# V of a batch's 64-row tail from two halves side by side in one stationary operand, and query weights staged in two parts

## Chip, cores and metric

The kernel runs on one core of one Trainium2 chip. The metric is the device time of one execution in microseconds; the runs shown are summarised by their median. The profile is of one further execution of the same program.

## What is computed

Three stages follow each other, for 8 batches of 576 positions. Retention attention gives x; a mixture of four attention experts with a gate that keeps two of them gives a new x; a token and channel mixing stage gives the output. Only the middle stage's projections of x matter here:

```python
logits = x @ w_gate                      # 512 -> 4
for e in range(E):                       # E = 4, head width 64
    q = x @ wq[e]; k = x @ wk[e]; v = x @ wv[e]
    scores = scale * (q @ k.transpose(0, 2, 1))
    ...                                  # causal softmax a, row sums
    ye = a @ v @ wo[e]
```

Products need more precision than one fast pass gives. So each operand is kept as two arrays, a rounded high part (h) and the remainder (l), and a product is three passes: h·h, h·l and l·h.

## The kernel before, in words

**Tiling.** The 576 positions of a batch are five chunks of 128, 128, 128, 128 and 64 rows (`ROWS`); the last one is the tail. `ret_values` (L164) makes x of one chunk in PSUM. VectorE scales it into `xt` (L190), ScalarE rounds it into `xh` (L192), and GpSimd subtracts the two into `xl` (L193). `xh` and `xl` hold a whole batch, four tiles of 128 contraction rows by 576 columns, with one buffer each (`XT`, L187). The routine ends by issuing, on SyncE's DMA queue, the loads of the chunk four places on (`loads`, L194 to L196).

**Projections.** `proj_qk` (L234) makes q or k of two experts for half of the positions; the weights are the stationary operand there. `proj_v` (L261) makes V and the gate's logits of one chunk: the stationary operand is the chunk of `xh` or `xl`, the moving operand is the 260 columns of V and gate weights. There are three passes of four contraction tiles, so 12 matmuls of 260 columns, for the 64-row tail (chunk 4, "v4") as for a 128-row chunk. ScalarE then copies the 256 columns of V (L276) and the 4 logits (L277) out of PSUM. `gate` (L279) works on the logits with a series of short VectorE instructions.

**Order.** TensorE's order is written out by hand. `SLOTS` (L45) says what goes beside each of the ten attention units of a batch; the next batch's tail is made in slot 8 ("R5") and its projections "v3 k01 v4 g" come in slot 9, so v4 is followed by that batch's gate. `ret_first` and `work` calls from L538 on do the same for batch 0, before attention starts. The other engines' queues are ordered by the framework's planner; TensorE's outputs go round a ring of eight PSUM buffers (`w`, `WB`).

**Weights.** The projection weights come in two staging tiles of the pool `w1s`: V and gate columns (512 to 772, `load_w1(512, NW1)`, L452), and the query and key columns (0 to 512, `load_w1(0, 512)`, L455) behind the first four chunks' loads. Of these, columns 0 to 256 serve the first pair of experts (k00, q00, k01), 256 to 512 the second (Q01, K10 and on, in attention's first slots). `split_w1` (L448) makes WH with ScalarE (L106) and WL with VectorE (L107), for the first 512 columns in four steps after the third chunk (L560 to L562). The pool is given back at L563.

Of the kernel before, what the change touches and what calls it, by code (L numbers as in the profile page):

```python
# [10 lines left out]
F32 = mybir.dt.float32  # L11
F32R = mybir.dt.float32r
# [3 lines left out]
AF = mybir.ActivationFunctionType  # L16
# [4 lines left out]
B, H, S, D = 8, 8, 576, 64  # L21
E, DM = 4, 512
# [4 lines left out]
NV = E * D + E  # L27
# [36 lines left out]
def tile_kernel(ctx: ExitStack, tc: tile.TileContext, qk, kv, w1, wo, wot, wd, cst, out):  # L64
    nc = tc.nc
    consts = ctx.enter_context(tc.tile_pool(name="consts", bufs=1))

    def pool(name, **kw):
        return tc.alloc_tile_pool(name=name, bufs=1, **kw)
# [11 lines left out]
    w1p = pool("w1p", side="right")  # L81
# [13 lines left out]
    WH = w1p.tile([128, 4, NW1], F32R, name="WH")  # L95
    WL = w1p.tile([128, 4, NW1], F32R, name="WL")
# [8 lines left out]
    def split(h, l, src):  # L105
        nc.scalar.activation(h, src, AF.Copy)  # L106
        MARK["split"] = nc.vector.tensor_sub(l, src, h)  # L107
# [24 lines left out]
    def half(x):  # L132
        return slice(x * 64, x * 64 + 64)
# [30 lines left out]
    def ret_values(b, c):  # L164

        R = ROWS[c]
        t, vp = QKT[b, c], VP[b, c]
        px = ps1.tile([128, 4, R], F32, name="w", bufs=WB, padded_shape=[128, 4, 128])
        for j in range(R // 64):
            sm = SM.pop((b, 2 * c + j))  # L170
            for x in range(4):
                for s in range(2):
                    nc.tensor.matmul(px[half(1 - s), x, half(j)], vp[half(s), j, x, :], sm[half(s), x, :],
                                     start=j == 0 and x == 0, stop=False, skip_group_check=True)
                yield
        for j in range(R // 64):
            k = 2 * c + j
            for x in range(4 if k else 0):
                for s in range(2):
                    nc.tensor.matmul(px[half(1 - s), x, half(j)], SB[k % 4][half(s), x, :], t[half(s), x, half(j)],  # L180
                                     start=False, stop=False, skip_group_check=True)
                yield
        for x in (QKT, KVT, VP):
            x.pop((b, c))
        cs = slice(c * C, c * C + R)
        if c == 0:
            XT[b] = (w1p.tile([128, 4, S], F32R, name="xh", bufs=1),  # L187
                     w1p.tile([128, 4, S], F32R, name="xl", bufs=1))
        xt = ret.tile([128, 4, R], F32, name="xt", bufs=2, padded_shape=[128, 4, 128])
        MARK["xt"] = nc.vector.tensor_mul(xt, px, gt[:, :, cs])  # L190
        xh, xl = XT[b]
        MARK["xh"] = nc.scalar.activation(xh[:, :, cs], xt, AF.Copy)  # L192
        MARK["xl"] = nc.gpsimd.tensor_sub(xl[:, :, cs], xt, xh[:, :, cs])  # L193
        nx = (b, c + LDB) if c + LDB < NCH else (b + 1, c + LDB - NCH)  # L194
        if nx[0] < B:
            loads(*nx)  # L196
# [64 lines left out]
    def proj_v(b, c):  # L261
        xh, xl = XT[b]
        if c == 0:
            VB[b] = att.tile([128, NCH, E, D], F32, name="V", bufs=2)
        V = VB[b]
        l = LG[b % 2]
        w0 = 512
        R = ROWS[c]
        cs = slice(c * C, c * C + R)
        ps = ps1.tile([128, NV], F32, name="w", bufs=WB, padded_shape=[128, 512])  # L270
        for x, W in ((xh, WH), (xh, WL), (xl, WH)):
            for kt in range(4):
                nc.tensor.matmul(ps[:R], x[:, kt, cs], W[:, kt, w0:w0 + NV], start=x is xh and W is WH and kt == 0,  # L273
                                 stop=x is xl and kt == 3)
        pv = ps[:R, :E * D].rearrange("p (e d) -> p e d", e=E)
        nc.scalar.copy(V[:R, c, :, :], pv)  # L276
        nc.scalar.activation(l[:R, c, :], ps[:R, E * D:], AF.Copy)  # L277
# [26 lines left out]
    def work(b, names):  # L304
        for n in names.split():
            x = b + n.islower()
            if x < B:
                if n in "Gg":
                    gate(x)
                elif n[0] == "T":  # L310
                    token_tile(ps1, 0, len(X2))
                elif n[0] == "F":
                    fuse(int(n[1]))
                elif n[0] in "Vv":
                    proj_v(x, int(n[1]))
                else:
                    proj_qk(x, int(n[1]), int(n[0] in "Kk"), int(n[2]))
# [94 lines left out]
    w1s = pool("w1s")  # L412
# [28 lines left out]
    wst = {}  # L441

    def load_w1(a, z):
        wst[a] = w1s.tile([128, 4, z - a], F32, name=f"wst{a}", bufs=1)
        nc.sync.dma_start(wst[a], w1.rearrange("(k p) n -> p k n", p=128)[:, :, a:z])

    def split_w1(a, k):
        t = wst[a]  # L448
        sl = slice(a, a + t.shape[2])
        split(WH[:, k, sl], WL[:, k, sl], t[:, k])  # L450

    load_w1(512, NW1)  # L452
    for c in range(1, LDB):
        loads(0, c)
    load_w1(0, 512)  # L455
    nc.sync.dma_start(tie, cst[:, o + 1088:o + 1088 + E * E].rearrange("p (a b) -> p a b", a=E))
    nc.sync.dma_start(ident, cst[:, 0:128])

# [73 lines left out]
    def fuse(p):  # L532
        acc = ps1.tile([128, DM], F32, name="w", bufs=WB)
        for kt, (th, wt) in enumerate(FW):
            mm3(acc, wt[:, 0, p, :], wt[:, 1, p, :], th[:, 0, :], th[:, 1, :], kt == 0, kt == 3)
        split(MH[:, p, :], ML[:, p, :], acc)
# [3 lines left out]
    for k in range(2):  # L540
        with tc.issue_after(MARK["xt"].ins), tc.issue_after(MARK["xh" if k else "S"].ins):
            split_w1(512, slice(2 * k, 2 * k + 2))
    with tc.issue_after(MARK["xl"].ins):
        scale()
    warm_up(WARM2)
# [13 lines left out]
    ret_first(0, 2, (0, 3), [(6, 7)])  # L559
    for k in range(4):  # L560
        with tc.issue_after(MARK["xt"].ins), tc.issue_after(MARK["xh"].ins):
            split_w1(0, k)  # L562
    w1s.release()  # L563
    work(-1, "v1")
    ret_first(0, 3, (0, 4), [(8,)])
    work(-1, "v2 k00")
# [86 lines left out]
    for t in range(nu + 1):  # L653
        b, k = divmod(t, 10)
        if b < B - 1:
            more, between, after = *SLOTS[k], ""
        else:
            b = B - 1
            more, between, after = LAST[t - 10 * b]
        if t < nu:  # L660
            at_scores(units[t])
            work(b, more)
            if units[t][2] == NCH - 1:
                at_norm(*units[t][:2])
        if t == nu - 1:
            assert not jobs[1]
            cvt.release()
            atk.release()
            zp = pool("zp")
        if between == "O":  # L670
            for o in outs:
                at_out(*o)
            outs = []
        ready, new = outs, []
        if t:
            at_trans(units[t - 1])
            ub, up, um = units[t - 1]
            if GROUPS[GRP[um]][-1] == um:
                new.append((ub, up, GRP[um]))
        outs = new  # L680
        if b < B - 1:
            if between[:1] == "R":
                c = int(between[1])
                x = b + 1
                def mid():
                    for o in ready:
                        at_out(*o)

                ret_step(x, c - 1, mid)
            else:  # L690
                outs = ready + outs
        else:
            work(b, between)
            for o in ready if t < nu else ready + outs:
                at_out(*o)
        work(b, after)


        i = int(t >= JOBS[0])
        x = t - JOBS[0] if i else t - 2  # L700
        while jobs[i] and (x + 1) / due[i] >= njobs[i] - len(jobs[i]) + 1 - 1e-6:
            with ExitStack() as es:
                for e in ("dve", "act"):
                    es.enter_context(tc.issue_after(MARK[e].ins))
                jobs[i].pop(0)()
        if t == nu - 11:
            assert not jobs[0]
            ret.release()
            w2 = pool("w2")
            WOH, WOL, MH, ML = [w2.tile([128, 2, DM], F32R, name=x) for x in ("WOH", "WOL", "MH", "ML")]  # L710
            wol = pool("wol")
            wa = pool("wa")
            fuse_load()
            load_o(0)
            load_o(1)
        if t == nu - 10:
            fuse_split(4)
        if t == nu - 8:
            fuse_split(0)
        if t == nu - 7:  # L720
            w1p.release()
            wa.release()
            w2b = pool("w2b")
            TK = w2b.tile([128, 9, 2, S], F32R, name="TK")
            wk1 = pool("wk1")
            for kt in KORD:
                nc.sync.dma_start(TK[:, kt].bitcast(F32), TD[kt])
# [257 lines left out]
```

## Time and profile before

| What | us |
|---|---|
| median of 3 runs | 880.44 |
| lowest and highest of the 3 | 877.99, 881.26 |
| the profiled execution | 879.58 |
| its span | 877.8 |

The span reaches from the first to the last instruction; 1.8 us of the profiled execution lie around it. TensorE is named PE in the profile (PEld for its weight loads), VectorE DVE, ScalarE ACT, GpSimd POOL and SyncE SP. "Idle before" is the time an engine stood still ahead of an instruction, with the work that ended last before it started; "issue" there means that the profile shows nothing it waited for.

### The profile page before, as it was taken

How to read it: one execution, taken by the hardware profiler on the slowest of the kernel's cores; microseconds unless marked ns; L12 is line 12 of the kernel's file. 1: busy time of each engine (PE TensorE's matmuls, PEld its weight loads, DVE VectorE, ACT ScalarE, POOL GpSimd, SP SyncE). 2: the span in 40 equal slices, each digit the busy share in tenths (PEclk: the TensorE clock that was granted, in tenths of full speed). 3: DMA queues.
4: the chain of work that ended last, by engine and by line, in shares of the span. 5: the costliest groups of instructions: out<-in, count | busy, mean ns of one | idle time of the engine just before them, and what ended most of it. 6: DMA issues, size and time to landing. Idle time of an engine off the chain costs nothing.

```text
span 877.8 us, 25574 instructions
## 1 busy us (share of the span) xinstructions
PE 859.2 (98%) x10072; PEld 795.2 (91%) x10072; DVE 622.0 (71%) x1729; ACT 454.6 (52%) x1258; POOL 218.7 (25%) x268
## 2 busy tenths in 40 slices
PE   6999999999999999999999999999999999999998
PEld 6989889888888989898789999999989999999998
DVE  4588787878788886876678777676377665766632
ACT  1366667666666766666576445353244533444320
POOL 3325253443525453341300012010210103001010
PEclk9899999999999999999999999999999999999999
DMA  9857677676867676548674442422525233241411
GB/s 317 246 155 239 171 221 199 194 224 187 255 169 222 202 211 179 160 108 238 185 265 170 83 111 47 120 37 61 141 57 139 62 96 93 34 124 25 100 34 54
DMA packets 140440, 130.30 MB, mean 148 GB/s; under 512 B 75808, under 2 KB 114976, under 8 KB 140320
## 3 DMA queue, kind: packets, MB, share of 16 engines
q1 hardware_dynamic: 140176, 128.39, 52.6%
q8 instruction: 79, 1.29, 0.6%
q0 software_dynamic: 144, 0.28, 0.2%
q14 instruction: 41, 0.34, 0.1%
HBM read 78.03 MB, written 32.00 MB: 125 GB/s over the span
## 4 chain that ended last, share of the span: by engine, by line
PE 88%; DMA 4%; DVE 3%; ACT 1%; issue 1%; POOL 1%; SPq 0%; ACTq 0%; DVEq 0%; POOLq 0%
PE acc L787 22%; PE w L245 11%; PE w L101 6%; PE w L102 6%; PE w L103 6%; PE w L335 6%; PE w L273 6%; PE w L401 5%; PE w L382 5%; PE w L787 3%; PE w L158 3%; PE w L143 3%; DMA kt<-qk 2%; DMA KK<-KN 1%; PE w L180 1%
## 5 line engine op out<-in xcount | busy, mean ns | idle before, releaser
L787 PE MATMUL acc<-TK,zh 128*128 128x288 f32 (+2 forms) x896 | 156.4, 296 | 0.5 <-ACT ob L405 0.5
L787 PEld LDWEIGHTS acc<-TK,zh 128*128 128x128 f32 x896 | 132.1, 189 | 1.2 <-issue 0.6
L343 ACT ACTIVATE P<-P,st 128x128 f32<-128x128 f32 (+4 forms) x160 | 95.4, 598 | 42.2 <-DVE st L338 41.9
L803 POOL TENSOR_TENSOR ul<-u,uh 128x576 fp32r<-128x576 f32 x16 | 24.2, 1531 | 309.6 <-ACT uh L802 309.6
L787 PE MATMUL acc<-TK,zl 128*128 128x288 f32 (+1 forms) x448 | 95.9, 295 | 0.0
L106 ACT ACTIVATE zh<-cs 128x512 fp32r<-128x512 f32 x64 | 40.3, 630 | 76.6 <-PE acc L787 61.4
L335 PE MATMUL w<-KK,U 128*64 128x288 f32 (+4 forms) x384 | 76.6, 327 | 1.5 <-DMA KK<-KN 1.4
L107 DVE TENSOR_TENSOR zl<-cs,zh 128x512 fp32r<-128x512 f32 x64 | 45.1, 705 | 43.2 <-ACT zh L106 42.5
L338 DVE CUSTOM_DVE_ANT_0 P<-w,cm 128x128 f32<-128x128 f32 (+4 forms) x160 | 71.1, 477 | 4.8 <-PE w L335 3.9
L787 PEld LDWEIGHTS acc<-TK,zl 128*128 128x128 f32 x448 | 72.4, 189 | 0.0
L626 ACT ACTIVATE cs<-cs,quarter 128x256 f32<-128x256 f32 x72 | 36.5, 507 | 55.4 <-DVE cs L624 55.2
L629 DVE SCALAR_TENSOR_TENSOR cs<-cs,x 128x512 f32<-128x512 f32 x72 | 50.7, 706 | 20.1 <-ACT cs L627 19.4
L382 PE MATMUL w<-ident,P 128*128 128x128 f32 (+2 forms) x480 | 60.1, 260 | 1.6 <-DVE sm L147 1.3
L335 PEld LDWEIGHTS w<-KK,U 128*128 128x128 f32 (+1 forms) x384 | 54.0, 171 | 8.0 <-DVE nwt L355 1.5
L193 POOL TENSOR_TENSOR xl<-xt,xh 128x512 fp32r<-128x512 f32 (+1 forms) x40 | 47.8, 1195 | 45.4 <-ACT xh L192 45.4
L479 POOL TENSOR_TENSOR r<-r,ex 128x192 f32<-128x192 f32 (+1 forms) x51 | 29.5, 578 | 116.2 <-ACT hl L480 42.0
L192 ACT ACTIVATE xh<-xt 128x512 fp32r<-128x512 f32 (+1 forms) x40 | 23.5, 589 | 66.9 <-DVE xt L190 66.8
L103 PE MATMUL w<-uh,CH 128*128 128x288 f32 x192 | 56.6, 295 | 0.0
L102 PE MATMUL w<-ul,CH 128*128 128x288 f32 x192 | 56.5, 294 | 0.0
L101 PE MATMUL w<-uh,CH 128*128 128x288 f32 x192 | 56.5, 294 | 0.0
L401 PE MATMUL w<-PT,V 128*64 128x192 f32 (+3 forms) x576 | 56.4, 325 | 0.0
L382 PEld LDWEIGHTS w<-ident,P 128*128 128x128 f32 (+2 forms) x480 | 47.1, 138 | 8.3 <-DVE sm L147 2.7
(153 smaller groups left out, 2340.4 us busy)
## 6 DMA issues: line engine op xcount, KB each, us to landing
KK<-KN SPq DMA_DIRECT2D x128, 144.0 KB
kt<-qk SPq DMA_DIRECT2D x32, 512.0 KB
kv<-kv SPq DMA_DIRECT2D x32, 512.0 KB
raw<-wd SPq DMA_DIRECT2D x43, 192.0 KB
xd<-xb SPq DMA_DIRECT2D x126, 64.0 KB
out<-u SPq DMA_DIRECT2D x28, 288.0 KB
u<-xd SPq DMA_DIRECT2D x28, 288.0 KB
td<-hl SPq DMA_DIRECT2D x27, 192.0 KB
```

The source lines that it names most:

```text
L101: nc.tensor.matmul(ps, ah, bh, start=first, stop=False)
L102: nc.tensor.matmul(ps, ah, bl, start=False, stop=False)
L103: nc.tensor.matmul(ps, al, bh, start=False, stop=last)
L245: nc.tensor.matmul(ps, W[:, kt, w0:w0 + 128], x[:, kt, sl], start=x is xh and W is WH and kt == 0, stop=x is xl and kt == 3)
L273: nc.tensor.matmul(ps[:R], x[:, kt, cs], W[:, kt, w0:w0 + NV], start=x is xh and W is WH and kt == 0, stop=x is xl and kt == 3)
L335: nc.tensor.matmul(ps[s][:R], U[:, s, rs], KK[:, s, x, j0:j1], start=x == 0, stop=x == 1)
L338: MARK["dve"] = nc.vector.tensor_tensor_reduce(Ps[s][:R, j0:j1], ps[s][:R], cm[:R, o + j0:o + j1], 1.0, st[:R, 0, s:s + 1] if i else 3.0e3 ...
L343: MARK["act"] = nc.scalar.activation(Ps[s][:R, :n], Ps[s][:R, :n], AF.Exp, bias=st[:R, last, s:s + 1], scale=-1.0, accum_out=SUM[p][:R, m, ...
L382: nc.tensor.transpose(tp[:w, j, :], Ps[s][:R, j * C:j * C + w], ident[:R, :R])
L401: nc.tensor.matmul(po[s * 64:s * 64 + 64, c0:], V[:ROWS[j], j, 2 * p + s, :], v, start=j == 0, stop=j == last, skip_group_check=True)
L629: nc.vector.scalar_tensor_tensor(z, cs, -1.0, x2[:, None, ds].to_broadcast([128, 2, 256]), op0=OP.mult, op1=OP.mult)
L787: nc.tensor.matmul(acc[d][j], A[:, dc], TK[:, kt, W, t0:t1], start=q == 0 and n == 0, stop=q == 8 and n == 2)
```

## The change

For the tail, `xl` becomes 64 columns wider. ScalarE writes the rounded tail of x a second time, into these columns, right behind the tail of `xl`, so that the two tails stand side by side as 128 columns. `proj_v` of the tail then takes these 128 columns as the stationary operand and makes two passes, with WH and WL, 8 matmuls of 260 columns. Rows 0 to 63 of the result hold the product of xl's tail, rows 64 to 127 that of xh's tail. ScalarE copies the upper rows to an SBUF tile `vt`, and VectorE adds this to the lower rows, once for V and once for the logits. The product of the two low parts, which was left out before, is now in the sum.

The staging tiles of the weights become two buffers of one name, each of 260 columns. Columns 0 to 256 are loaded where 0 to 512 were; columns 256 to 512 are loaded into the first buffer, after the V weights in it have been split. The four split steps stay where they were, with 2 contraction tiles of 256 columns each in place of one of 512. The pool `vtp` takes the place of the staging pool and is given back with `ret`.

```diff
@@ ret_values
-                     w1p.tile([128, 4, S], F32R, name="xl", bufs=1))
+                     w1p.tile([128, 4, S + 64], F32R, name="xl", bufs=1))
...
         MARK["xl"] = nc.gpsimd.tensor_sub(xl[:, :, cs], xt, xh[:, :, cs])
+        if R == 64:
+            nc.scalar.activation(xl[:, :, S:], xt, AF.Copy)
@@ proj_v
+        if R == 64:
+            for W in (WH, WL):
+                for kt in range(4):
+                    nc.tensor.matmul(ps, xl[:, kt, S - 64:], W[:, kt, w0:w0 + NV], start=W is WH and kt == 0,
+                                     stop=W is WL and kt == 3)
+            t = vtp.tile([64, NV], F32, name="vt", bufs=1)
+            nc.scalar.activation(t, ps[64:], AF.Copy)
+            tv, pv = [x[:, :E * D].rearrange("p (e d) -> p e d", e=E) for x in (t, ps[:64])]
+            nc.vector.tensor_add(V[:64, c, :, :], pv, tv)
+            nc.vector.tensor_add(l[:64, c, :], ps[:64, E * D:], t[:, E * D:])
+            return
@@ load_w1
-        wst[a] = w1s.tile([128, 4, z - a], F32, name=f"wst{a}", bufs=1)
+        wst[a] = w1s.tile([128, 4, z - a], F32, name="wst", bufs=2, padded_shape=[128, 4, NV])
@@ the startup
-    load_w1(0, 512)
+    load_w1(0, 256)
...
             split_w1(512, slice(2 * k, 2 * k + 2))
+    load_w1(256, 512)
...
-            split_w1(0, k)
+            split_w1(k // 2 * 256, slice(k % 2 * 2, k % 2 * 2 + 2))
     w1s.release()
+    vtp = pool("vtp")
...
             ret.release()
+            vtp.release()
```

## Rows read from the trace of the kernel before

**Rows 1.** The page: span, busy time by engine, share of the span, instructions.
```profile
span 877.8 us, 25574 instructions
PE 859.2 (98%) x10072; PEld 795.2 (91%) x10072; DVE 622.0 (71%) x1729; ACT 454.6 (52%) x1258; POOL 218.7 (25%) x268
```

**Rows 2.** Busy time by stretch: start:end, length, each engine's busy time, granted clock.
```profile
0.00:45.00 45.00, 37.20 (x801) 35.21 (x802) 22.93 (x48) 12.99 (x34) 15.72 (x24) 0.92 0.87 280
45.00:96.00 51.00, 50.66 (x875) 45.75 (x875) 42.13 (x144) 33.25 (x109) 20.24 (x28) 1.00 0.66 189
...
352.00:404.00 52.00, 51.74 (x811) 46.75 (x811) 41.30 (x145) 34.36 (x115) 18.38 (x28) 1.00 0.51 137
```

**Rows 3.** The chain that ended last: share of the span by engine.
```profile
PE 88%; DMA 4%; DVE 3%; ACT 1%; issue 1%; POOL 1%; SPq 0%; ACTq 0%; DVEq 0%; POOLq 0%
```

**Rows 4.** Waits of PE over the span: in total, times, longest.
```profile
PE w L180 <- issue: 4.0, 2, 2.9
...
PE w L382 <- DVE sm L147: 1.3, 5, 0.3
```

**Rows 5.** That chain in batch 0's startup: start, length, work.
```profile
38.06 1.44 PE w L273 x12
39.50 1.60 PE w L245 x12
41.10 1.44 PE w L273 x12
42.53 0.39 PE w L335 x4
```

**Rows 6.** That chain around v3, k01, v4 of batch 1.
```profile
83.95 1.43 PE w L273 x12
85.38 1.82 PE w L245 x12
87.20 1.43 PE w L273 x12
```

**Rows 7.** The tail's matmuls and loads, by form, 38 to 45 us.
```profile
L273 PEld LDWEIGHTS w<-WL,xh x8: 133/160/190, 38.3 to 41.6; 128*128 128x128 f32 x4, 128*64 128x64 f32 x4
```

**Rows 8.** ACT in time order: tail rounding, tail V and logits.
```profile
35.98 0.42 ACT L192 ACTIVATE xh<-xt 128x256 fp32r<-128x256 f32 x1 [1.53 <-DVE xt L190]
...
42.57 0.36 ACT L276 COPY V<-w 64x256 f32<-64x256 f32 x1 [1.02 <-PE w L273]
42.84 0.17 ACT L277 ACTIVATE lg<-w 64x4 f32<-64x4 f32 x1
```

**Rows 9.** DVE in time order: an add from PSUM, then the gate's start.
```profile
31.80 0.41 DVE L162 TENSOR_TENSOR S<-w,S 128x256 f32<-128x256 f32 x1
...
43.03 0.18 DVE L282 TENSOR_REDUCE gmx<-lg 128x5 f32<-128x20 f32 x1 [1.00 <-ACT lg L277]
```

**Rows 10.** All engines in time order around batch 1's v4.
```profile
85.62 0.74 POOL L193 TENSOR_TENSOR xl<-xt,xh 128x256 fp32r<-128x256 f32 x1
...
85.86 0.78 ACT L343 ACTIVATE P<-P,st 64x576 f32<-64x576 f32 x1 [0.77 <-DVE st L338]
...
89.14 0.17 DVE L282 TENSOR_REDUCE gmx<-lg 128x5 f32<-128x20 f32 x1 [0.41 <-ACT lg L277]
...
94.00 0.93 DVE L259 SCALAR_TENSOR_TENSOR U<-w,U 64x288 fp32r<-64x288 f32 x2 [0.86 <-ACT U L256]
...
94.45 0.82 PE L382 MATMUL w<-ident,P 64*128 64x64 f32 x10
```

**Rows 11.** SyncE's DMA issues in time order: weights, then the loads behind.
```profile
7.88 0.43 SPq L445 DMA_DIRECT2D wst<-w  x1
...
14.58 0.33 SPq L120 DMA_DIRECT2D kv<-kv  x1
21.22 0.33 SPq L117 DMA_DIRECT2D kt<-qk  x1
```

**Rows 12.** The weight splits at startup in time order: V's last, then 512 columns.
```profile
11.73 1.35 DVE L107 TENSOR_TENSOR WL<-wst,WH 128x520 fp32r<-128x520 f32 x1 [0.62 <-ACT WH L106]
...
27.22 2.17 ACT L106 ACTIVATE WH<-wst 128x512 fp32r<-128x512 f32 x4
...
27.87 4.01 DVE L107 TENSOR_TENSOR WL<-wst,WH 128x512 fp32r<-128x512 f32 x4 [1.22 <-ACT WH L106]
```

**Rows 13.** PE resuming after two startup gaps, in time order.
```profile
20.74 0.27 PE L180 MATMUL w<-kt,S 64*64 64x64 f32 x2 [2.85 <-issue]
...
25.07 0.37 PE L180 MATMUL w<-kt,S 64*64 64x64 f32 x2 [1.17 <-issue]
```

**Rows 14.** Busy time up to each gap, and the stretches behind (columns as above).
```profile
0.00:17.90 17.90, 14.11 (x349) 12.86 (x350) 8.03 (x13) 3.91 (x7) 6.04 (x15) 1.00 0.92 318
...
0.00:23.90 23.90, 17.27 (x476) 15.83 (x476) 11.28 (x19) 4.54 (x8) 8.07 (x17) 0.95 0.94 310
...
20.00:25.00 5.00, 3.16 (x127) 2.96 (x126) 2.89 (x6) 0.63 (x1) 1.90 (x2) 0.64 0.97 275
25.00:30.00 5.00, 4.93 (x108) 4.68 (x109) 3.16 (x4) 3.04 (x7) 2.61 (x2) 0.67 0.72 186
```

**Rows 15.** Instruction queue: whole span (packets, MB), then from 18 to 19 us.
```profile
q8 instruction: 79, 1.29, 0.6%
...
q8 instruction: 1, 0.02, 7.0%
```

## The prediction

> **What bounds the kernel now.** I read the page's busy times first: TensorE is busy for 859.2 of 877.8 us, and no other engine passes 71% [rows 1]. An average can hide stages, so the busy time by stretch comes next. Before attention starts TensorE idles for 45.0 - 37.2 = 7.8 us; in a whole batch of attention, 45 to 96 us, for 0.34 us, and in the last one that still projects, 352 to 404 us, for 0.26 us [rows 2]. The chain that ended last says the same, with 88% of it on TensorE [rows 3]. The waits name what is left: the largest by far is 4.0 us of "issue" in two gaps at startup, and the largest on another engine's work in the attention stage is 1.3 us in five pieces [rows 4]. So a matmul taken out of attention should come off the time nearly whole, and an instruction added to another engine costs only what it makes TensorE wait. The startup is a case of its own.
>
> **Part 1, four matmuls fewer in each tail.** In the chain, v3 (128 stationary columns) takes 1.44 us from 38.06 to 39.50 and v4 (64 columns) 1.44 us from 41.10 to 42.53, 12 matmuls each [rows 5]; in batch 1 the two take 1.43 us each [rows 6]. That is 119 ns a matmul, and a full stationary operand costs no more than a half one. So the tail's 8 matmuls of 128 columns take 8 x 119 = 0.95 us in place of 1.43, 0.48 us less, and in eight batches 8 x 0.477 = 3.8 us. All eight tails lie before 404 us, seven of them inside full attention slots and batch 0's in a stretch where the chain goes from matmul to matmul. Each moves work behind it up by as much.
>
> The weight loads do show the width: 133 ns at the least for 64 columns, 188 to 190 ns for 128 [rows 7]. They lie beside the matmuls, so I cost the difference at nothing; the cover is the 119 ns pitch, which both widths hold. Were the loads what sets the pitch, 8 x 188 = 1.50 us against 12 x 133 = 1.60 us would leave 0.1 us a batch, 0.8 us in all. The Trainium skill ("TensorE: Matmul & The Clock Gate", section "LDWEIGHTS (loading the stationary operand)") says that a load takes as many cycles of 1.2 GHz as it has columns, and this speaks against the change: by it, as an estimate, eight loads of 107 ns are 0.21 us more than twelve of 53 ns, 1.7 us more over eight batches if loads set the pace. The trace agrees that width lengthens a load, with other numbers, but the equal 1.44 us say that here the load does not end last.
>
> **Part 2, the second writing of xh's tail.** One ScalarE instruction of 128x256 elements a batch, like the first writing, 0.42 us [rows 8], 3.4 us in all. Queued behind it is the exponential of the tail's attention unit, which before stood 0.77 us idle for VectorE at this place; and GpSimd's xl tail, which v4 needs too, ends only at 85.62 + 0.74 = 86.36, after the copy would (from 85.1 to 85.5) [rows 10]. So it is hidden, at nothing. Without that cover it would cost 0.42 us a batch.
>
> **Part 3, getting V out of PSUM.** Before: ScalarE 0.36 us for V and 0.17 us for the logits [rows 8]. After: one ScalarE copy of 64x260, about 0.37 us, then on VectorE an add of 256 columns from PSUM, about 0.41 us by the 128x256 add, and an add of 4 columns, about 0.18 us by the gate's first short instruction [rows 9]. The trace has no such add of 64 rows and 4 columns, hence "by". VectorE gets 0.6 us more a batch, 4.7 us in all. The new wait is VectorE's for ScalarE's copy; queued behind it are the gate and the next units' score reductions. Before, the gate waited there too, 1.00 us in batch 0 and 0.41 us in batch 1 [rows 9, 10], and since the logits' own ScalarE copy drops out, the gate starts at about +0.3 us. Later VectorE has a pause of 0.86 us at 93.1 to 94.0, where it waits for ScalarE's part of U [rows 10], and there the delay ends. The PSUM buffer is held for some 0.5 us longer; its next user is the eighth output after v4, the transposes at 94.45, six microseconds after v4's end at 88.6 [rows 6, 10]. Bounds of part 3: 0 if all is covered, 8 x 0.6 = 4.7 us if every added VectorE instant reaches TensorE. The trace is near the lower end (1.3 us for all such waits of five pieces); I take 0.3 us.
>
> **Part 4, weights in two parts.** The first half, 512 KB, is issued where 1 MB was, at 7.88 us. The second waits for the last split of the V weights, 11.73 + 1.35 = 13.08 us; on SyncE's queue it stands behind the tail's kv load at 14.58 us, so it goes out at about 15 to 16 us, and the load behind it is not due before 21.22 us [rows 11]. It is wanted by ScalarE's third split, about 27.22 + 2 x 0.54 = 28.3 us [rows 12], some 12 us later. The bytes are the same, the four steps split the same number of elements, so ScalarE's 2.17 us and VectorE's 4.01 us stay [rows 12]. k00, q00 and k01 need only the first two steps now, some 2 us earlier than before, but TensorE was not waiting there. Cost: nothing in the likely case.
>
> What can move is the supply of instructions. TensorE's 20,144 instructions came in 79 packets [rows 1, 15], about 255 each, some 128 matmuls with their loads. The two "issue" gaps of 2.85 and 1.17 us [rows 13] stand at the 349th and the 476th matmul, 127 apart, and while TensorE stood in the first, one such packet moved between 18 and 19 us [rows 14, 15]. So I read them as waits for the next packet while the data loads fill the DMA engines (shares of 0.92 and 0.94 [rows 14]). Behind the first gap the granted clock falls to the lower level, 1.2 GHz: means of 0.64 and 0.67 in two stretches of 5 us are 3.6 + 3.3 = 6.9 us of it [rows 14]; less the second gap that is 5.7 us of work at half speed, which costs about 2.9 us more. The Trainium skill ("Runtime: NRT & Kernel Launch", section "Instruction fetch mechanics") has the same 256-instruction blocks but says that fetching is hidden by the time instructions take to issue; here the rows show 4 us that were not. Early in the startup half a megabyte less now stands in the queue, in rows of 1 KB and not 2 KB, and the rest follows behind. I can't say which way a packet's place moves; bounds are -4.0 us (both gaps gone), -7 us with the clock, and +3 us (the first gap again). I take 0.
>
> **Sum.** -3.8 + 0.3 = -3.5 us. The profiled execution's 879.58 us (span 877.8 and 1.8 around it) gives 876.1; it lies 0.86 us below the median of 880.44, which gives 876.9. The mean of the three runs and the profiled one is 879.8, so I say **876.2**.
>
> **The rivals.**
> (a) The startup's instruction wait shrinks. For it: smaller pieces ahead of the packet. Against: the same bytes fill the queue at 15 to 20 us. Half of the gaps and of the clock's loss would be -3.5 us: 872.7; the case spans 870 to 875.
> (b) The saving is given back: the added 0.6 us of VectorE in each batch shows as a wait of the next transposes, or the packet comes later. Half of 4.7 us is 2.4: 878.6, span 877.6 to 881. Against it are the pauses named in part 3.
> (c) Loads set the pitch once they are wide, so only 0.8 us is saved: 879.0. Here the change doesn't do what it says. The skill's rule of part 1, worked out with its own figures, would make it 1.7 us slower. The equal 1.44 us speak against both.
> (d) Slower: the second half of the weights lands late, because its issue waits for a free staging buffer behind SyncE's other loads. ScalarE and VectorE then stand in the third split, and x of the fourth chunk, queued behind it on VectorE, is late for TensorE. It decides from a landing at 28.3 us; for a loss of over 0.5% it has to eat 3.8 + 4.4 = 8.2 us, a landing at about 36.5 us. At 40 us: 28.3 to 40 is 11.7, less 3.8: 888. The 12 us of margin speak against it.
>
> **How the numbers follow.** 0.5% of 880.44 is 4.4 us, about what a measurement of this kernel can tell from no change; faster means below 876.0. My forecast has 0.55 and spans 874.8 to 877.6, split by that bound into 0.20 faster and 0.35 same. (a) has 0.22, all faster; (b) 0.14 and (c) 0.04, same; (d) 0.05, slower. So faster 0.42, same 0.53, slower 0.05. For 8 in 10, I leave out the lower third of (a), the upper third of (b), part of (c) and all of (d): 872.8 to 879.8.
>
> **What would show it.** Right: each L273 group of the tail has 8 matmuls in about 0.95 us; TensorE's busy time is some 3.8 us lower; its waits in attention stay under 1 us a batch; VectorE's gate starts at most 0.6 us later behind v4. Wrong: tail groups at 140 ns or more a matmul (c); a new wait of transposes or scores on VectorE in each batch (b); other "issue" gaps or clock in the first 30 us (a or b); an idle ScalarE ahead of the third split (d).

## The result, and the profile after

The changed kernel takes 886.72 us (median of 7, 881.91 to 887.82) against 878.72 us for the kernel before in the same comparison: a ratio of 1.0076 [1.0049, 1.0103] (ratios here are of the means, with 95% intervals). By the medians it is slower by 8 us; the forecast was 876.2, and its range ended at 879.8. The profiled execution took 886.5 us, 6.9 us more than the profiled one of before (879.58).

The page's busy times (as in [rows 1]) and the chain's shares by engine (as in [rows 3]) show at once that TensorE got no more work: it has the 32 matmuls fewer that were meant. VectorE has the 16 short instructions more, and ScalarE is busy 3.3 us longer, as forecast (3.4). What grew is "issue", from 1% to 2% of the chain. TensorE's busy time isn't the 3.8 us lower that was named as a sign of being right: it is 859.5 us after 859.2. Work at the lower clock counts as busy for longer, 1.4 us of it at startup and up to 1.7 us behind 275 us (both below); the rest was not traced.

```profile
span 884.7 us, 25540 instructions
PE 859.5 (97%) x10040; PEld 795.7 (90%) x10040; DVE 623.1 (70%) x1745; ACT 457.9 (52%) x1258; POOL 219.6 (25%) x268
...
PE 90%; DMA 3%; issue 2%; DVE 2%; SPq 1%; POOL 1%; ACT 1%; POOLq 0%; DVEq 0%; ACTq 0%
```

Busy time by stretch (start:end, length, busy time of each engine, granted clock, DMA share, GB/s; the first and the fourth answer [rows 2]). TensorE's idle time in a stretch is the length less the first busy time: 0.80 us at 45 to 96 (0.34 before), and then 2.29, 2.17 and 1.80 us. From 275 to 280 us the mean granted clock is 0.66 as well.

```profile
45.00:96.00 51.00, 50.20 (x867) 45.28 (x866) 42.54 (x150) 33.70 (x109) 20.20 (x28) 1.00 0.66 192
96.00:147.00 51.00, 48.71 (x866) 43.87 (x865) 40.14 (x141) 32.27 (x106) 20.27 (x29) 1.00 0.69 195
...
250.00:300.00 50.00, 47.83 (x846) 42.70 (x845) 39.65 (x127) 30.70 (x101) 22.44 (x31) 0.97 0.67 198
...
352.00:404.00 52.00, 50.20 (x800) 45.20 (x796) 40.89 (x147) 33.88 (x110) 20.26 (x32) 1.00 0.48 128
...
275.00:280.00 5.00, 4.07 (x40) 3.89 (x39) 3.48 (x11) 1.62 (x5) 3.27 (x4) 0.66 0.83 264
```

TensorE's waits between 45 and 405 us, after (line and what it waited for; total, times, longest). The wait for VectorE's `sm` is to the tenth what [rows 4] had, 1.3 us in five pieces. The lines of "issue" are 4.8 + 2.3 + 2.0 = 9.1 us.

```profile
PE w L158 <- issue: 4.8, 3, 1.9
PE w L180 <- issue: 2.3, 2, 1.6
PE w L143 <- issue: 2.0, 1, 2.0
PE w L395 <- DVE sm L147: 1.3, 5, 0.3
PE w L143 <- DMA kt<-qk: 0.5, 1, 0.5
```

The same view of the kernel before, in the same window, has two short "issue" waits, 0.9 us in all:

```profile
PE w L143 <- issue: 0.6, 1, 0.6
PE w L245 <- issue: 0.3, 1, 0.3
```

The chain that ended last, after (start, length, what): besides the two startup gaps there is now about one gap a batch, some 50 us from the next (one of 0.71 us at 171.07 is not among the lines here). All stand in the same place of a batch's program, among the 64x64 matmuls of the retention part (`L143`, `L158`, `L173`, `L180`).

```profile
19.74 2.22 issue
24.05 2.13 issue
...
119.00 2.03 issue
...
221.98 1.41 issue
...
274.02 1.91 issue
...
328.41 1.57 issue
...
380.55 1.53 issue
```

And the chain around the tails, after, in batch 0 (answering [rows 5]) and batch 1 (answering [rows 6]). v4, now `L276`, takes 0.96 us for eight matmuls, as forecast:

```profile
42.31 0.96 PE w L276 x8
43.27 0.39 PE w L348 x4
...
88.81 0.96 PE w L276 x8
```

**Where the 7 us went in.** The last batch's tail is the point at which all eight savings are behind. Before, its v4 runs from 394.28 for 1.43 us; after, from 401.96 for 0.95 us. So it ends 402.91 - 395.71 = 7.20 us later, and from there to the end nothing more is lost (the span is 6.9 us longer). The pieces: "issue" gaps between 45 and 405 us, 9.1 - 0.9 = +8.2; seven tails at -0.48, -3.4; the startup, first matmul behind batch 0's v4 at 43.27 in place of 42.53, +0.74, with batch 0's saving in it; the clock behind the gap at 274 us, an estimate of (1 - 0.66) x 5 us = up to +1.7; TensorE's waits for the loads and for `ob` in attention -0.4. That sums to 6.8 of the 7.2 us.

### The profile page after: what moved, and what is told of

The parts are those of the page before. It is cut to its first block, busy times and chain, and to the rows that moved or that the text cites. A ratio compares the mean times of both kernels' runs of the same rounds, so it can differ in the third digit from the quotient of the medians.

```text
span 884.7 us, 25540 instructions
## 1 busy us (share of the span) xinstructions
PE 859.5 (97%) x10040; PEld 795.7 (90%) x10040; DVE 623.1 (70%) x1745; ACT 457.9 (52%) x1258; POOL 219.6 (25%) x268
## 4 chain that ended last, share of the span: by engine, by line
PE 90%; DMA 3%; issue 2%; DVE 2%; SPq 1%; POOL 1%; ACT 1%; POOLq 0%; DVEq 0%; ACTq 0%
PE acc L803 22%; PE w L247 11%; PE w L348 7%; PE w L101 6%; PE w L102 6%; PE w L103 6%; PE w L414 5%; PE w L395 5%; PE w L286 5%; PE w L803 3%; PE w L158 3%; PE w L143 3%; PE w L180 1%; PE w L173 1%; DMA og<-gd 1%
```

## What the gaps are, and two theories

The prediction had read the two startup gaps as waits for the next packet of instructions, 127 matmuls apart [rows 13 to 15]. The same arithmetic done over the whole trace is what it lacked. I counted TensorE's rows (loads, matmuls and semaphore waits in order of time). The two startup gaps of before stand at rows 705 and 961, 256 apart. In the changed kernel the five gaps of the chain above stand at 4289, 7873, 9665, 11457 and 13249, and the one of 0.71 us at 6081: from each to the next it is 1792 = 7 x 256. A batch is 1789 rows long before and 1782 after (eight instructions fewer for four matmuls, one wait more). So a block border comes back to nearly the same place of each batch, and every instruction taken out ahead of a border moves it to a later place of the program.

**Packet theory.** Removing instructions shifts the borders of 256. At a bad place the next packet comes late, and TensorE stands 1 to 2 us in each batch. If so, the same kernel with another number of instructions must lose the gaps, and the kernel before, shifted, must get them.

**Rivals.** *Tail:* the new tail itself, its wait for ScalarE's copy or the second writing, sets something late further on. *Weights:* the split load moves the startup. And inside the packet theory: *loads*, the packet queues behind the data loads; *wait*, the request for it stands behind TensorE's wait for VectorE's scores.

## The experiments

Ratios are against the kernel before in the runs of the same chip, with 95% intervals. Diffs show the lines that matter; cuts are marked.

**Less work without the change's new waits.** The kernel before, with one of the tail's three passes left away:

```
-        for x, W in ((xh, WH), (xh, WL), (xl, WH)):
+        passes = ((xh, WH), (xh, WL)) if R == 64 else ((xh, WH), (xh, WL), (xl, WH))
+        for i, (x, W) in enumerate(passes):
...
```

> The kernel before, with one edit: the tail's V leaves out the pass of xl's tail with WH, so it has 8 matmuls in place of 12 (that part of V is missing). No second writing of xh, no adds on VectorE, weights staged as before. Packet theory (TensorE's instructions come in blocks of 256; 8 instructions fewer in each batch shift every later block border against the loads of keys and values, and the packet then queues behind them): slow like the changed kernel, 881 to 888 us, with an issue gap of 1 to 2 us in most batches. Tail theory (VectorE's add, ScalarE's copy or the wide stationary operand cost the time): 3.8 us faster than before, 875 us. Weights theory (staging in two parts costs it): 875 us as well.

883.27 us, 1.0050 [1.0027, 1.0072]. Eight matmuls in place of twelve, no second writing, no new wait, the old weights: and it is slower. In its profiled execution, at 879.6 us one of its fastest, TensorE's waits between 45 and 405 us have 5.7 us of "issue" where before has 0.9:

```profile
PE w L180 <- issue: 3.0, 2, 1.5
PE w L158 <- issue: 2.7, 3, 1.3
```

The tail theory falls: taking the instructions out is enough.

**The instructions put back.** The changed kernel, with four matmuls of 32 columns, whose result is overwritten, ahead of each tail group:

```
+            for kt in range(4):
+                nc.tensor.matmul(ps[:, :32], xl[:, kt, S - 64:], WH[:, kt, w0:w0 + 32], start=True, stop=True)
```

> The changed kernel, with four added matmuls of 32 columns ahead of each tail's V, into the same PSUM buffer, overwritten by what follows: 8 instructions more in each batch, so the block borders stand nearly where they stood before the change. Packet theory: the issue gaps in attention go, and the time falls to 875 to 878 us although work is added (eight times four matmuls, about 1 us). Tail theory and weights theory: 887 to 888 us, the changed kernel's time and about 1 us more.

877.88 us, 0.9977 [0.9954, 1.0001]. With more work than the changed kernel it is about 9 us faster than that was, each against the kernel before. Its waits between 45 and 405 us:

```profile
PE w L143 <- DMA kt<-qk: 1.3, 3, 0.7
...
PE w L247 <- issue: 0.2, 1, 0.2
```

The gaps are gone with all of the change's new operations in place.

**The weights alone.**

```
-    load_w1(0, 512)
+    load_w1(0, 256)
...
+    load_w1(256, 512)
...
```

> The kernel before, with only the weights staged in two parts; the tail's V as before. Packet theory: TensorE's instructions are the same, so 877 to 881 us, same as before. Weights theory: 884 to 888 us. Tail theory: same as before.

878.02 us, 0.9987 [0.9968, 1.0007]: no difference that shows, and the weights theory falls. One gap of 1.2 us stands in its trace at 323 us, where before has its 0.6.

**The kernel before, shifted.** Nothing but its warm-up differs: 40 matmuls of 160 columns in place of 50 of 128, 20 instructions fewer at the start.

```
-WARM = 50
+WARM = 40
...
-            nc.tensor.matmul(pw, warm, warm, start=True, stop=True)
+            nc.tensor.matmul(pw[:, :m], warm[:, :128], warm[:, :m], start=True, stop=True)
```

> The kernel before, with 40 warm-up matmuls of 160 columns in place of 50 of 128: the same array time, 20 instructions fewer at the very start, all else as before. Packet theory: every block border moves 20 instructions later in the program, beyond where the changed kernel's gaps begin (about 17 to 19 behind the place before), so an issue gap of 1 to 2 us shows in most batches and the time is 885 to 890 us. Tail and weights theories: 877 to 881 us, same as before.

884.72 us, 1.0062 [1.0037, 1.0088], 0.3 us short of the range expected. The chain of this kernel, which has all the old code, shows the pattern of the changed one:

```profile
167.95 1.23 issue
...
219.80 1.27 issue
...
272.16 1.15 issue
...
324.41 1.32 issue
...
376.93 1.39 issue
```

This settles that the place of the borders is the cause: it is worth 0.6% by itself, with no change to the work of attention. Why a place is bad is another question, which the next runs ask.

**Is the packet late behind the data loads?** The changed kernel with half the bytes of every load from batch 1 on:

```
-        nc.sync.dma_start(t, qk[b, :, o:o + 8 * R].rearrange("p (h r) -> p h r", h=8))
+        nh = 8 if b == 0 else 4
+        nc.sync.dma_start(t[:, :nh], qk[b, :, o:o + nh * R].rearrange("p (h r) -> p h r", h=nh))
...
```

> The changed kernel, but from batch 1 on each load of keys and values brings only its first half (the scores take q for k and the values k for v, so the result is another; TensorE's instructions, their order and their sizes are the same). If the instruction packet waits behind the loads in the DMA engines, a half burst lets it through sooner: the gaps of 0.9 to 2.3 us in attention shrink to 0.5 us or less. If a fetch is late by itself, wherever loads stand (a block of small matmuls is simply shorter than a fetch), the gaps stay between 0.9 and 2.3 us.

878.63 us in one execution, but five gaps stayed: 5.9 us of "issue" between 45 and 405 us, where the changed kernel has 9.1. At the gap of 217.81 us the DMA view of this kernel, from 215 to 216 us and then from 216 to 217 us, reads:

```profile
DMA packets 3, 0.01 MB, mean 10 GB/s; under 512 B 1, under 2 KB 2, under 8 KB 2
...
DMA packets 31, 0.02 MB, mean 19 GB/s; under 512 B 30, under 2 KB 30, under 8 KB 30
...
q8 instruction: 1, 0.02, 5.8%
```

and its chain, at the same place:

```profile
217.81 1.15 issue
218.97 0.33 PE w L184 x4
```

The engines are all but idle for more than a microsecond, and TensorE's packet moves only in the second window. So at this gap no load in the engines holds it up in the microsecond before it moves; that it was asked for late is what this leaves, and isn't seen directly. The gaps didn't shrink to 0.5 us, and the theory of the loads as the main cause falls. Since their sum went down by 3.2 us, the loads may have a part in it; one execution doesn't show that.

**Does the request stand behind the wait for the scores?** The changed kernel, where the retention values take a constant from batch 1 on:

```
-                    nc.tensor.matmul(px[half(1 - s), x, half(j)], vp[half(s), j, x, :], sm[half(s), x, :],
+                    nc.tensor.matmul(px[half(1 - s), x, half(j)], vp[half(s), j, x, :], sm[half(s), x, :] if b == 0 else tri[half(s), :],
```

> The changed kernel, but from batch 1 on the retention's values take the constant mask in place of the masked scores (so the result is another): TensorE's instructions and sizes stay, but the block of small matmuls ahead of each gap no longer waits for VectorE's masked scores, which end about 0.9 us before TensorE gets there. The half loads have shown that the packet is late without a burst of loads, so something else sets when it is asked for. If TensorE's queue asks for the next packet only when it has got past this wait, the gaps of 0.9 to 2.3 us fall to half or less. If they stay, this wait is not what the request stands behind.

883.81 us in one execution. The gaps stayed, 8.2 us of them between 45 and 405 us:

```profile
PE w L158 <- issue: 4.3, 3, 1.9
PE w L180 <- issue: 3.9, 2, 2.4
```

So the scores aren't shown to be it. The run settles less than it was meant to: in its trace, as in the changed kernel's, 35 of the weight loads of the line edited (`L173`) wait for a semaphore from batch 1 on, and the load ahead of the gap at row 9665 still waits for VectorE's. The value waited for isn't in the trace. What the edit took away is the use of the scores, not the wait, so a request that stands behind this wait, or behind another of TensorE's in the block, is not ruled out.

**The changed kernel at other places.** Only its warm-up is cut into more and narrower matmuls, with the same number of columns (64 x 100, 80 x 80, 100 x 64, 120 x 53, 150 x 43 in place of 50 x 128). It adds 28, 60, 100, 140 and 200 instructions ahead of everything else. One of the five as a diff, the others alike:

```
-WARM = 50
+WARM = 100
...
-            nc.tensor.matmul(pw, warm, warm, start=True, stop=True)
+            m = 64 if n == WARM else 128
+            nc.tensor.matmul(pw[:, :m], warm, warm[:, :m], start=True, stop=True)
```

> As the one with 80 warm-up matmuls, but with 64 of 100 columns: borders 28 instructions earlier, at -19, -9, 1, 11, 21, 31 and 41 in the seven batches. Packet theory: no gap in the first four, gaps of 1 to 2 us in the last three (at about 274, 328 and 380 us in the program's time), and a time between: 878 to 882 us. Every other theory: gaps and time as in the changed kernel, 885 to 888 us.

879.02 us, 1.0019 [0.9994, 1.0044]. The border drifts ten instructions further with each batch; as expected the gaps at this border begin with the fifth (1.12 us at 270.11, then 322.20 and 373.77 in the chain). Not expected were gaps of 0.4 to 0.9 us at another border, rows 3009, 4801 and 8385.

> The changed kernel with 80 warm-up matmuls of 80 columns in place of 50 of 128: the same array time, 60 instructions more at the start, so that each later border of a block stands 60 instructions earlier in the program. Counted from the place where the kernel before had it in batch 0, the border that gapped stands at -51, -41 and so on to +9 in the seven batches, ahead of the bad region (from about 17). Packet theory: no gap of 1 us in attention unless one of the other six borders of a batch has moved into a bad region; 874 to 877 us, which is the change's own gain of 3.8 us at last. Every other theory: 885 to 888 us, the changed kernel's time.

876.31 us, 0.9977 [0.9957, 0.9997], 0.2 us of "issue" between 45 and 405 us.

> As the one with 80 warm-up matmuls, but with 100 of 64 columns: borders 100 instructions earlier, at -91 to -31. Packet theory: no gap at this border, 874 to 877 us; if another border of the seven comes into a bad region, its gap shows at another place of the batch and the time is 880 us or more. Every other theory: 885 to 888 us.

875.24 us, 0.9968 [0.9952, 0.9984], and none there.

> The changed kernel with 120 warm-up matmuls of 53 columns: borders 140 instructions earlier. The gap at the border studied stays away. By the shift of 100 the first gap of the startup went and the second stayed at 2.9 us; by 140 the second may move off the small matmuls as well. 873 to 876 us if no other border comes into a bad region; with one, a gap of 1 us or more in most batches and 880 us or more.

874.54 us, 0.9951 [0.9931, 0.9971]: faster than both kernels, the best of the study. Its waits between 45 and 405 us have no "issue" at all (the two longest lines here); only one startup gap is left on its chain ahead of 600 us, of 3.27 us.

```profile
PE w L395 <- DVE sm L147: 1.3, 5, 0.3
PE w L143 <- DMA kt<-qk: 0.9, 1, 0.9
...
```

> The changed kernel with 150 warm-up matmuls of 43 columns: borders 200 instructions earlier, so the border studied stands where the one before it stood less 56: nearly a whole block round. If the place of the border is all that counts, some of a batch's seven borders come again near the bad region 256 instructions further on (the border studied moved to -191 to -131, the next one to +65 to +125, beyond the region from 17 to 69 that gapped); at 65 to 69 a gap may show in the first of the seven batches, and in the others none. 874 to 878 us with at most one gap of 1 us; 880 us or more if the bad region reaches on beyond 69.

880.15 us, 1.0024 [1.0005, 1.0043]. Here I was wrong: the gaps are back, now at the border behind (row 2753 and on, every 1792). At one of these borders, row 9921, TensorE stands 2.0 us that the view puts down to ScalarE's `xh`, so the two causes can't be told apart there. The good stretch is narrower than I had thought.

```profile
PE w L158 <- issue: 2.8, 2, 1.6
...
PE w L180 <- issue: 1.8, 2, 0.9
```

**The kernel before, given the same favour** (100 warm-ups of 64 columns):

> The kernel before with 100 warm-up matmuls of 64 columns in place of 50 of 128: the same shift of borders that gave the changed kernel its best time (875.2 us, 0.9968 of before). If that gain is the change's own 3.8 us, the kernel before stays at 877 to 879 us with it, or falls by the 1 to 2 us that the shift saves at startup, 876 to 878. If the shift alone makes the gain, this kernel reaches 875 us too, and the change is worth nothing.

877.79 us, 0.9988 [0.9973, 1.0003], no "issue" between 45 and 405 us. This is the fair partner of the changed kernel with the same warm-up: two kernels that differ by the change and have no gaps there. The profiled spans are 874.6 and 870.9 us, 3.7 us apart; the medians 877.79 and 875.24, 2.5 us apart (the runs of before beside them had medians of 879.64 and 878.16, so the ratios, 0.9988 and 0.9968, are only 0.2% apart and their intervals overlap). So the comparison of whole executions doesn't show the forecast saving of 3.8 us clear of noise. The tails measure the change without the startup: v4 of batch 1 and v4 of batch 5 start 291.52 - 88.01 = 203.51 us apart without the change, and with it 289.06 - 87.47 = 201.59. That is 1.92 us over four tails, 0.48 each in the mean, 0.33 to 0.56 from tail to tail; as TensorE's waits for loads in this stretch are 1.0 us without the change and 0.6 with it, the mean is close to the forecast partly by luck. The tails themselves take 1.43 and 0.95 us. From the chain of the kernel before with 100 warm-ups:

```profile
88.01 1.43 PE w L273 x12
...
291.52 1.43 PE w L273 x12
```

From the chain of the changed kernel with 100 warm-ups:

```profile
87.47 0.95 PE w L276 x8
...
289.06 0.95 PE w L276 x8
```

**When a packet is late.** With the rows counted, each packet of TensorE's instruction queue can be set beside its block. This table (worked out from the traces; us) is for the block that ends at row 9665, in the middle of the run. Its gaps reach from the start of one row to the start of the next, and so are some 0.2 us longer than the idle time in the chain:

```
kernel             packet starts,     TensorE runs    left for    gap at
                   after entry of     through the     the packet  row 9665
                   the block          block in
before                  1.13             4.45           3.32        none
before, shifted         3.50             4.50           1.00        1.36
changed                 3.84             4.02           0.18        2.12
changed, padded        -0.18             4.44           4.62        none
changed, +28            3.44             4.54           1.10        1.34
changed, +60            0.23             4.44           4.21        none
changed, +100           0.63             5.65           5.02        none
changed, +140           1.37             5.66           4.29        none
```

In the 28 gaps of over 0.5 us that I set out this way (in seven kernels, from 60 to 340 us) TensorE goes on 2.2 to 2.7 us after its packet's start. The same count over all fourteen kept traces, with the packets taken in order, has 675 borders between 45 and 405 us: at the 41 with less than 1.8 us left for the packet there was a gap of over 0.5 us each time, and at the 611 with 2.5 us or more left TensorE stood idle for 0.3 us at most. So two things make a border good: an early start of the packet, or a block that takes long. In a block of 4.4 us a start 1.1 us after TensorE's entry was early enough, one of 3.0 us or more was not; in one of 5.66 us a start as late as 3.1 us did no harm; in blocks of 2.0 to 2.4 us starts of 0.7 to 1.0 us were too late. Why it starts 2 to 4.4 us late at some places stays open: the loads aren't the main cause, the run without the scores doesn't settle its question, and no run showed what the request stands behind.

## Why the prediction was wrong, by its own steps

**What bounds the kernel: right.** TensorE is the bound, and a matmul taken out of attention comes off whole. In the pair without gaps 0.48 us came off in each tail, in the mean of four.

**Part 1: right in size.** 0.96 and 0.95 us for eight matmuls of 128 columns, where 0.95 was forecast; the pitch of 119 ns held and rival (c), loads as the pitch, falls: it would have left 0.1 us a batch, and 0.48 was measured.

**Part 2: right.** The second writing takes 0.40 us, and the exponential behind it still stands idle for VectorE, 0.46 us in place of the 0.77 of [rows 10]. ScalarE after, in order of time:

```profile
86.60 0.40 ACT L195 ACTIVATE xl<-xt 128x256 fp32r<-128x256 f32 x1
87.47 0.78 ACT L356 ACTIVATE P<-P,st 64x576 f32<-64x576 f32 x1 [0.46 <-DVE st L351]
```

**Part 3: right, at no cost that shows.** VectorE after, in order of time (answering [rows 9, 10]): the adds take 0.41 and 0.14 us. The gate's first instruction starts 1.00 us after v4's end (89.77), before 0.51 us after it; that is 0.5 us later, in batch 0 0.6 (43.27 to 44.40, before 42.53 to 43.03), where I had 0.3. TensorE's waits for VectorE's scores didn't change (1.3 us in five), so the 0.3 us that I put on it is not to be seen.

```profile
90.26 0.41 DVE L281 TENSOR_TENSOR V<-w,vt 64x256 f32<-64x256 f32 x1
90.59 0.14 DVE L282 TENSOR_TENSOR lg<-w,vt 64x4 f32<-64x4 f32 x1
90.77 0.17 DVE L295 TENSOR_REDUCE gmx<-lg 128x5 f32<-128x20 f32 x1
```

**Part 4: right.** The second half goes out at 15.89 us, where I had 15 to 16, and the four splits take what they took in [rows 12], with the same 1.22 us of idle time ahead of VectorE's; rival (d) has nothing for it. SyncE, then ScalarE and VectorE after:

```profile
15.89 0.38 SPq L458 DMA_DIRECT2D wst<-w  x1
...
28.19 2.18 ACT L106 ACTIVATE WH<-wst 128x512 fp32r<-128x512 f32 x4
28.84 4.00 DVE L107 TENSOR_TENSOR WL<-wst,WH 128x512 fp32r<-128x512 f32 x4 [1.22 <-ACT WH L106]
```

**The step that failed is the last one of the change's working, "What can move is the supply of instructions".** It named the right thing and looked at it in one place only, the startup, and only at what stands ahead of a packet there. I bounded it by -7 and +3 us and took 0. It was not seen that the change takes eight instructions out of each batch, that blocks are counted through the whole program, and that with this every later border moves against the code: in attention, where before had only 0.9 us of "issue", the packets were in time because of where the borders fell. The step was worth +8.2 us in attention, with up to 1.7 us of clock behind one gap. A count of TensorE's rows would have shown before's own gap of 0.6 us in attention to stand on a border as well (row 11457 = 961 + 41 x 256), and the drift from batch to batch that the change speeds up from 3 instructions to 10.

**The rivals.** (b) had "or the packet comes later" in it, but priced it at half of 4.7 us and gave it no place; (a) didn't come, the startup was 0.74 us longer with two gaps as before; (c) and (d) fell. Of the four only (d), at 888 us, ended well above the kernel before, by a mechanism that didn't occur; that its time lies near the measured 886.72 is luck. The rule of the Trainium skill that I had set against the rows, that fetching is hidden or mostly so ("Runtime: NRT & Kernel Launch", section "Instruction fetch mechanics"), holds in this trace at 42 of the 48 borders between 45 and 405 us and fails at six, where 9.1 us were not hidden. Its block of 256 instructions agrees with every gap that was counted.

## What to carry to other kernels

On an engine that is busy 98% of the time, the number of its instructions is itself a parameter: a change that adds or removes some ahead of a loop moves every block border behind it, and here that alone put the changed kernel anywhere from 0.5% faster to 0.8% slower than before, more than the work that was saved. Look for "issue" waits in the view of the bound engine, count its rows to see whether they are a multiple of 256 apart, and before judging a small change time it together with a few numbers of filler instructions at the start. Where small matmuls follow each other for a whole block, that block is the place at risk, as in the gaps shown here.

## What the runs showed of the hardware that I had not expected

- A packet of TensorE's instructions had to start some 2.4 us ahead of the moment at which TensorE reached it: at the gaps it moves for 0.9 to 1.5 us, and TensorE goes on 2.2 to 2.7 us after its start. The blocks of 256 instructions ahead of the gaps, mostly 64x64 matmuls, run in 2.0 to 4.5 us, so that little of a block is left to hide it.
- The packet of a block may start as TensorE enters the block ahead or up to 4.4 us later at a gap (changed kernel, 118.66 us, for an entry at 114.29), 5.2 us at a border without one. In the run with half loads the DMA engines were all but idle when the late one of the gap at 217.81 us started. What decides it isn't known.
- A gap of 1.91 us in the middle of attention was followed by a stretch with a mean granted clock of 0.66 over 5 us, between the full 2.4 GHz and the half of it. The others in that trace, of 0.7 to 2.0 us, were not.
- In some executions the first matmuls behind the warm-up run at the lower clock and in others not: between 14 and 16 us the granted clock is 1.00 in the kernel before and 0.50 in the changed one. The first six take 0.98 and 1.57 us, the next 32 1.10 and 1.93 us. The changed kernels with 60 and 200 instructions more had about 0.98 and 1.10 again, so the change alone doesn't bring it; of the nine traces of kernels with the change, one execution each, four have it, of the five without it none. In the profiled execution of the changed one it is 1.4 us of its startup.
